# Seven block products in place of eight for h times w_down, in the second half of the rows

## The chip, the cores and the metric

The kernel runs on one core of one Trainium2 chip. The metric is the device time of one execution in microseconds (us); the kernel before took 1466.3 us (median of 3 runs, 1465.88 to 1466.41). The engines are named PE (matrix products; PEld is its loading of weights, the stationary operand), DVE (vector), ACT (scalar), POOL and SP; SP issues nearly all DMAs.

## The reference

With S = 2048 rows, D = 576 and F = 4608, all in float32:

```python
xn = _layernorm(x)                       # x: 1 x 2048 x 576
A  = irfft2(rfft2(xn) * (w_r + 1j * w_i))
h  = sigmoid(xn @ w_gate) * (xn @ w_up)  # 2048 x 4608
out = x + A + h @ w_down                 # w_down: 4608 x 576
```

## The kernel before

**Precision.** A float32 operand is held as two parts, hi and lo, each of which PE multiplies fast. A product is made of three: hi by hi, hi by lo, lo by hi. ACT makes a hi part by a copy, DVE the lo part by a subtraction.

**Staging.** The rows come in two halves of 1024 (`p` = 0, 1), each with two chunks of 512 (`c`) and eight row tiles of 128 (`m`). F comes in 36 blocks of 128 columns (`f`). A unit is one block f of one half: u = 36 p + f, 0 to 71. The normed rows of a half lie transposed in `X`, in hi and lo parts.

**Gate and up.** The first two blocks of each half are made by `plain` (L588), eight block products in two calls. All others are made by `unit` (L607): the 2 x 2 blocks (chunk by half of D, half of D by gate or up) need seven products by sums made beforehand (`PRODS`), each of seven matmuls of 128 x 512 (`prod`, L574, matmul at L576). `unit` puts sigmoid and product together in `y` (128 x 2 x 512), and from y come `hh` and `hl`, the hi and lo parts of h (L662, L663). The four tiles of X that are free are filled with sums beside products that read the others (`fill`, L365).

**Down.** Two units make a pair j = 0 to 17 of each half. `down` (L665) makes for one row tile the product of the pair's h with w_down, twelve matmuls of 128 x 288 (L676) into a pair of PSUM banks; `add` (L679) adds it to `acc` on DVE (L681). The eight row tiles of a pair are spread over the next two units, two after the fifth product of a unit and two after the sixth (`spots`). The pairs of banks (`pair`, L143) are two deep and shared with the spectral part.

**Spectral part.** The transform runs in three stages, `phase1b` (L386), `phase2` (L439) and `phase3` (L483), each of 16 tiles, as generators that are stepped once after each product in units 39 to 71 (`begin`, `aside`). Each issues its loads three steps ahead of its first use.

**Weights.** In the first half, `make_w` and `make_d` (L224, L257) load the raw weights, split them and form their sums, and store the parts in DRAM; in the second half `get_w` (L250) and `get_d` (L269) load the parts. A unit's weights `w` are two deep: unit u + 1's are loaded into the buffer of unit u - 1.

**Order.** `turn` (L811) steps the weights' generators, the additions that are due and the side jobs after each product; `ends` holds the last steps of a unit, which are done in the next one. The framework then orders each engine's instructions by priority and readiness, so that the spectral part's matmuls stand between and inside products. At the end of unit 71, eight row tiles of the last pair remain, each stored as it is done.

Of the kernel before, what the change touches and what calls it, by code (L numbers as in the profile page):

```python
# [33 lines left out]
NX = 7  # L34

# [95 lines left out]
def spectral_glu_kernel(ctx: ExitStack, tc: tile.TileContext, x, w_r, w_i, w_gate, w_up, w_down, out):  # L131
# [38 lines left out]
    wdsp = [tc.dram_tile([P, 2 * D], F32, name=f"wdsp{f}") for f in range(NF)]  # L170

# [5 lines left out]
    accp = ctx.enter_context(tc.tile_pool(name="accp", bufs=1))  # L177
    wpool = ctx.enter_context(tc.tile_pool(name="wpool", bufs=1))
    hp = ctx.enter_context(tc.tile_pool(name="hp", bufs=1))

# [8 lines left out]
    def room(k):  # L189
        fp.close()  # L190
        R["pool"] = pool = fp.enter_context(tc.tile_pool(name=f"p{k}", bufs=1, reuse_waits="tile"))
        return pool
# [30 lines left out]

    def make_w(f):  # L224

        raw = RAW[f]
        WS[f] = w = wpool.tile([P, NX, 5, P], F32R, tag="w", name=f"w{f}", bufs=2)
# [12 lines left out]

    def make_p(f):

        raw = RAW[f]
        WS[f] = w = wpool.tile([P, NX, 5, P], F32R, tag="w", name=f"w{f}", bufs=2)
        for i in (2, 0):
            yield from parts(w, raw[:, i:i + 2], i, 2)
        nc.sync.dma_start(wsp[f][:, :4 * 5 * P], f32(w[:, :4]).rearrange("p a k m -> p (a k m)"))
        yield

    def get_w(u):  # L250
        f = u % NF
        WS[u] = w = wpool.tile([P, NX, 5, P], F32R, tag="w", name=f"w{u}", bufs=2)
        for i in [WB[b] for _, _, b in PRODS] if f >= G else (3, 2, 0, 1):
            nc.sync.dma_start(f32(w[:, i]).rearrange("p k m -> p (k m)"), wsp[f][:, i * 5 * P:(i + 1) * 5 * P])
            yield

    def make_d(f):  # L257
        st = wpool.tile([P, D], F32, tag="std", name=f"std{f}", bufs=1)
        nc.sync.dma_start(st, w_down[f * P:(f + 1) * P, :])
        for _ in range(4):  # L260
            yield
        WD[f] = w = wpool.tile([P, 2, D], F32R, tag="wd", name=f"wd{f}", bufs=4)
        placed(nc.scalar.activation(w[:, 0], st, AF.Copy))
        yield
        nc.vector.tensor_tensor(w[:, 1], st, f32(w[:, 0]), op=OP.subtract)
        nc.sync.dma_start(wdsp[f], f32(w).rearrange("p a d -> p (a d)"))
        yield

    def get_d(u):  # L269
        WD[u] = w = wpool.tile([P, 2, D], F32R, tag="wd", name=f"wd{u}", bufs=4)  # L270
# [83 lines left out]
    def sums(p, m):  # L354
# [5 lines left out]
        rem_parts(p, m, 3, "rm12", 2)  # L360
# [20 lines left out]
    def new_acc(p, m):  # L381
        t = p * TPP + m
        acc[t] = accp.tile([P, D], F32, tag=f"acc{m}", name=f"acc{t}")
# [185 lines left out]
    H = {}  # L569
# [13 lines left out]
    def new_h(u):  # L583
        hh, hl = (hp.tile([P, 2, CW], F32R, tag=k, name=f"{k}{u}", bufs=3) for k in ("hh", "hl"))
# [22 lines left out]
    def unit(u, beside):  # L607


        g, v, y = (hp.tile([P, 2, CW], F32, tag=k, name=f"{k}{u}", bufs=1) for k in ("g", "v", "y"))  # L610
# [31 lines left out]
        hh, hl = new_h(u)  # L642
        if u == LAST - 1:

            nc.vector.tensor_tensor(y[:, 1], y[:, 1], g[:, 1], op=OP.mult)
            nc.scalar.activation(hh[:, 1], y[:, 1], AF.Copy)
            nc.vector.tensor_tensor(hl[:, 1], y[:, 1], f32(hh[:, 1]), op=OP.subtract)
# [3 lines left out]
            nc.scalar.activation(hh[:, 0], y[:, 0], AF.Copy)  # L651
            nc.vector.tensor_tensor(hl[:, 0], y[:, 0], f32(hh[:, 0]), op=OP.subtract)
# [5 lines left out]
        def first():  # L658
# [3 lines left out]
        ends.extend([first, lambda: nc.scalar.activation(hh, y, AF.Copy),  # L662
                     lambda: nc.vector.tensor_tensor(hl, y, f32(hh), op=OP.subtract)])  # L663

    def down(p, j, m):  # L665
# [4 lines left out]
        for g in range(G):  # L670
            u = p * NF + j * G + g
            hh, hl = H[u]
            w = WD[u]
            for l, k in ((hh, 0), (hh, 1), (hl, 0)):
                for b in range(2):
                    nc.tensor.matmul(pd[:, b, :HD], l[:, c, cols], w[:, k, b * HD:(b + 1) * HD],  # L676
                                     start=g == 0 and l is hh and k == 0, stop=g == G - 1 and l is hl)
# [12 lines left out]
        return add  # L690

# [117 lines left out]
    wd = iter(())  # L809

# [14 lines left out]
    for p in range(PAIRS):  # L825
# [38 lines left out]
        for f in range(G, NF):  # L864
            u = p * NF + f

            spots = {4: 2, 5: 2}
            if u + 1 < LAST:
                make = make_w(u + 1) if u + 1 < NF else get_w(u + 1)
            wd = make_d(u) if u < NF else get_d(u)  # L870
# [5 lines left out]
            def beside(i):  # L876
                nonlocal step
                for _ in range(spots.get(i, 0)):
                    if pend:
                        adds.append(down(*pend.pop(0)))  # L880
                if i < 0:
                    return
                turn(2 if u + 1 < NF else 1)
# [6 lines left out]
            finish(make, wd)  # L890
            if u + 2 < NF:
                load_raw(u + 2)
            if f % G == G - 1:

                pend = [(p, f // G, (m + TPC) % TPP if u == LAST - 1 else m) for m in range(TPP)]
# [5 lines left out]
    while pend:  # L901
        down(*pend.pop(0))()
    fp.close()
# [20 lines left out]
```

## Time and profile before

| | |
|---|---|
| time, median of 3 runs | 1466.3 us |
| time of the profiled execution | 1467.37 us |
| its span, first to last instruction | 1465.3 us |
| mean granted TensorE clock | 0.999 |
| HBM read, written | 188.01 MB, 118.42 MB |
| DMA packets, mean rate | 150742, 210 GB/s |

The profile is one execution. A group's row gives line, engine, operation, output and inputs, shapes and count; then its busy time in us and the mean of one in ns; then the idle time of the engine before these instructions, and who ended it. A matmul's end is modelled, and matmuls overlap. A row of a chain gives start, duration and what it was. A row of a stretch (window) gives its limits and length, then for PE, PEld, DVE, ACT and POOL the busy time with the count, then the granted clock, the share of the DMA engines and GB/s. A row of waits gives the total in us, how often, and the longest.

### The profile page before, as it was taken

How to read it: one execution, taken by the hardware profiler on the slowest of the kernel's cores; microseconds unless marked ns; L12 is line 12 of the kernel's file. 1: busy time of each engine (PE TensorE's matmuls, PEld its weight loads, DVE VectorE, ACT ScalarE, POOL GpSimd, SP SyncE). 2: the span in 40 equal slices, each digit the busy share in tenths (PEclk: the TensorE clock that was granted, in tenths of full speed). 3: DMA queues.
4: the chain of work that ended last, by engine and by line, in shares of the span. 5: the costliest groups of instructions: out<-in, count | busy, mean ns of one | idle time of the engine just before them, and what ended most of it. 6: DMA issues, size and time to landing. Idle time of an engine off the chain costs nothing.

```text
span 1465.3 us, 21488 instructions
## 1 busy us (share of the span) xinstructions
PE 1447.4 (99%) x8244; PEld 1275.7 (87%) x8244; DVE 935.7 (64%) x1608; ACT 591.3 (40%) x1021; POOL 5.1 (0%) x21
## 2 busy tenths in 40 slices
PE   7999999999999999999999999999999999999998
PEld 5888888888888888888888888888888889889898
DVE  6888977777777777765455555456666554554544
ACT  5634443444334434453334444434444433333321
POOL 0000000000000000000000000000000000000000
PEclk9999999999999999999999999999999999999999
DMA  6578766666666666666755546477767576744532
GB/s 207 213 258 267 253 225 226 220 217 218 239 235 233 228 223 231 220 206 212 259 179 192 189 155 196 145 229 244 246 217 255 198 246 214 234 158 160 182 109 65
DMA packets 150742, 307.86 MB, mean 210 GB/s; under 512 B 14064, under 2 KB 77808, under 8 KB 145776
## 3 DMA queue, kind: packets, MB, share of 16 engines
q1 hardware_dynamic: 149712, 305.18, 62.0%
q8 instruction: 65, 1.06, 0.3%
q10 hardware_dynamic: 928, 1.31, 0.2%
q14 instruction: 37, 0.30, 0.1%
HBM read 188.01 MB, written 118.42 MB: 209 GB/s over the span
## 4 chain that ended last, share of the span: by engine, by line
PE 92%; DMA 3%; DVE 2%; SPq 1%; ACT 1%; issue 1%; ACTq 0%; DVEq 0%
PE po L676 30%; PE pB L576 22%; PE pE L576 16%; PE pA L576 14%; PE pe L533 2%; PE pd L423 2%; PE pa L434 1%; PE pc L478 1%; PE py L504 1%; PE pb L462 1%; DMA raw<-in_B_w_gate 1%; DMA xt<-in_A_x 0%; PE pz L516 0%; SPq L277 0%; PE pf L408 0%
## 5 line engine op out<-in xcount | busy, mean ns | idle before, releaser
L676 PE MATMUL po<-wd,hh 128*128 128x288 f32 x2304 | 401.7, 296 | 1.6 <-DVE acc L681 1.3
L576 PE MATMUL pB<-X,w 128*128 128x512 f32 x1484 | 381.8, 393 | 1.7 <-ACT w L217 0.9
L681 DVE TENSOR_TENSOR acc<-acc,po 128x576 f32<-128x576 f32 x288 | 215.9, 752 | 226.1 <-PE po L676 225.6
L676 PEld LDWEIGHTS po<-wd,hh 128*128 128x128 f32 x2304 | 343.9, 188 | 16.0 <-DVE acc L681 3.5
L576 PEld LDWEIGHTS pB<-X,w 128*128 128x128 f32 x1484 | 270.8, 188 | 53.5 <-ACT pB L623 1.4
L576 PE MATMUL pE<-X,w 128*128 128x512 f32 x1064 | 274.2, 392 | 0.0
L576 PE MATMUL pA<-X,w 128*128 128x512 f32 x1008 | 260.9, 394 | 0.2 <-DVE X L379 0.2
L676 PE MATMUL po<-wd,hl 128*128 128x288 f32 x1152 | 246.1, 294 | 0.0
L576 PEld LDWEIGHTS pE<-X,w 128*128 128x128 f32 x1064 | 193.2, 188 | 34.4
L576 PEld LDWEIGHTS pA<-X,w 128*128 128x128 f32 x1008 | 188.1, 190 | 37.8 <-DVE X L379 0.7
L676 PEld LDWEIGHTS po<-wd,hl 128*128 128x128 f32 x1152 | 186.4, 189 | 0.0
L217 ACT ACTIVATE w<-raw 128x768 fp32r<-128x768 f32 (+1 forms) x106 | 100.4, 948 | 108.5 <-PE pE L576 88.2
L640 ACT ACTIVATE g<-pB 128x512 f32<-128x512 f32 x68 | 40.6, 598 | 188.1 <-PE pB L576 188.1
L663 DVE TENSOR_TENSOR hl<-y,hh 128x1024 fp32r<-128x1024 f32 x67 | 82.1, 1225 | 31.2 <-ACT hh L662 30.2
L219 DVE TENSOR_TENSOR w<-raw,w 128x512 fp32r<-128x512 f32 (+1 forms) x106 | 81.9, 773 | 5.1 <-ACT w L217 4.7
L660 DVE TENSOR_TENSOR y<-y,g 128x1024 f32<-128x1024 f32 x67 | 82.0, 1224 | 3.6
L662 ACT ACTIVATE hh<-y 128x1024 fp32r<-128x1024 f32 x67 | 70.7, 1055 | 2.8 <-DVE y L660 2.2
L623 ACT ACTIVATE pB<-pA 128x512 f32<-128x512 f32 x68 | 39.6, 582 | 79.5 <-PE pA L576 79.5
L630 ACT ACTIVATE v<-pB 128x512 f32<-128x512 f32 x68 | 40.6, 597 | 67.8 <-PE pB L576 67.5
L637 DVE TENSOR_TENSOR y<-v,pE 128x512 f32<-128x512 f32 x68 | 46.5, 685 | 29.9 <-ACT v L636 28.8
L659 DVE TENSOR_TENSOR y<-v,pE 128x512 f32<-128x512 f32 x67 | 45.9, 685 | 27.6 <-PE pE L576 27.5
L183 DVE TENSOR_TENSOR al<-pd,ah 64x290 fp32r<-64x290 f32 x64 | 29.3, 457 | 40.7 <-ACT ah L182 40.2
(146 smaller groups left out, 1258.4 us busy)
## 6 DMA issues: line engine op xcount, KB each, us to landing
w<-wsp SPq DMA_DIRECT2D x246, 320.0 KB
wsp<-w SPq DMA_DIRECT2D x34, 2240.0 KB
wdsp<-wd SPq DMA_DIRECT2D x36, 576.0 KB
wd<-wdsp SPq DMA_DIRECT2D x36, 576.0 KB
std<-in_B_w_down SPq DMA_DIRECT2D x36, 288.0 KB
raw<-in_B_w_gate SPq DMA_DIRECT2D x72, 128.0 KB
raw<-in_B_w_up SPq DMA_DIRECT2D x72, 128.0 KB
sc<-x SPq DMA_DIRECT2D x16, 290.0 KB
```

The costliest lines, as they stand in the source:

```text
L217: placed(nc.scalar.activation(o[:, :, :3, :], src, AF.Copy))
L219: placed(nc.vector.tensor_tensor(o[:, :, 3:, :], src[:, :, :KT, :], f32(o[:, :, :KT, :]), op=OP.subtract))
L576: nc.tensor.matmul(bank, w[:, sw, :], X[:, x, sx, :], start=start and j == 0, stop=stop and j == len(STEPS) - 1, skip_group_check=skip)
L630: nc.scalar.activation(v[:, 0], bank["B"], AF.Copy)
L637: nc.vector.tensor_tensor(y[:, 1], v[:, 1], bank["E"], op=OP.add)
L640: nc.scalar.activation(g[:, 1], bank["B"], AF.Sigmoid)
L659: nc.vector.tensor_tensor(y[:, 0], v[:, 0], bank["E"], op=OP.add)
L660: nc.vector.tensor_tensor(y, y, g, op=OP.mult)
L662: ends.extend([first, lambda: nc.scalar.activation(hh, y, AF.Copy), lambda: nc.vector.tensor_tensor(hl, y, f32(hh), op=OP.subtract)])
L663: lambda: nc.vector.tensor_tensor(hl, y, f32(hh), op=OP.subtract)])
L676: nc.tensor.matmul(pd[:, b, :HD], l[:, c, cols], w[:, k, b * HD:(b + 1) * HD], start=g == 0 and l is hh and k == 0, stop=g == G - 1 and l ...
L681: nc.vector.tensor_tensor(a, a, pd[:, :, :HD], op=OP.add)
```

## The change

In the second half of the rows, for the pairs j = 1 to 15 (`SEVEN`), h times w_down is made as 2 x 2 blocks (chunk by unit of the pair, unit of the pair by half of D) by seven products. `factor` forms the sums of h in place in the `y` tiles and splits them (`halves`); `make_t` forms the sums of w_down in the first half and stores them in `tsp`. `seven` makes an item in two steps of six matmuls, one step after each product of a unit, and adds it to a running sum: three of the seven go to `acc`, four to `qs`, which `gather` puts together in unit 70. The pairs 0, 16 and 17 of the second half stay with `down`. Unit 38 takes all eight row tiles of pair 0; pair 16 goes to units 70 and 71. Weights of w_down come by block of 128 x 288 (`load_f`).

The buffers are laid out anew: `acc` is one tile, the pools of the spectral part lie on the right side, and a second pool (`lower`) is closed after unit 38 and opened with other tiles. From unit 39 on all units use one tile of `w`: slot by slot, the next unit's weights are loaded into it after the product that read the slot.

```diff
+SEVEN = range(1, NF // G - 2)
...
+    tsp = {j: tc.dram_tile([P, 4 * 2 * HD], F32, name=f"tsp{j}") for j in SEVEN}
...
+    AC = accp.tile([P, TPP, D], F32, name="acc")
...
+    def lower(k):
+        lp.close()
+        L["pool"] = lp.enter_context(tc.tile_pool(name=f"l{k}", bufs=1, reuse_waits="tile"))
...
+    def new_w(u):
+        if u > NF + G:
+            WS[u] = WS[NF + G]
+        else:
+            pool = L["pool"] if u % 2 else wpool
+            WS[u] = pool.tile([P, NX, 5, P], F32R, tag="w", name=f"w{u}", bufs=1)
+        return WS[u]
...
+        if g == 1 and j in SEVEN:
+            yield from make_t(j)
+
+    def make_t(j):
+        b = STD[j].rearrange("p g (b d) -> p (g b) d", b=2)
+        t = R["pool"].tile([P, 4, HD], F32, tag="xa", name=f"wt{j}", bufs=TPC)
+        nc.vector.tensor_tensor(t[:, :2], b[:, 1::2], b[:, :2], op=OP.subtract)
+        nc.vector.tensor_tensor(t[:, 2], b[:, 3], t[:, 0], op=OP.subtract)
+        nc.vector.tensor_tensor(t[:, 3], b[:, 2], t[:, 2], op=OP.subtract)
+        yield
+        th, tl = (R["pool"].tile([P, 4, HD], F32R, tag="xa", name=f"{k}{j}", bufs=TPC) for k in ("wth", "wtl"))
+        split(th, tl, t)
+        for i, v in enumerate((th, tl)):
+            nc.sync.dma_start(tsp[j].rearrange("p (k a d) -> p k a d", k=4, a=2)[:, :, i], f32(v))
+        yield
...
+        late_h = u >= NF + G
+        pool, tag = (hp, "y") if not late_h or u % 4 == (NF + G) % 4 else (L["pool"], f"y{u % 4}")
+        Y[u] = y = pool.tile([P, 2, CW], F32, tag=tag, name=f"y{u}", bufs=1)
...
-        ends.extend([first, lambda: nc.scalar.activation(hh, y, AF.Copy),
-                     lambda: nc.vector.tensor_tensor(hl, y, f32(hh), op=OP.subtract)])
+        ends.append(first)
+        if not late_h:
+            hh, hl = new_h(u)
+            ends.extend([lambda: nc.scalar.activation(hh, y, AF.Copy),
+                         lambda: nc.vector.tensor_tensor(hl, y, f32(hh), op=OP.subtract)])
...
+    ROUND = (("A11", "B11", "Q1"), ("A12", "B21", "C11"), ("A22", "T4", "C21"), ("S1", "T1", "Q5"),
+             ("S3", "T3", "Q7"), ("S2", "T2", "Q6"), ("S4", "B22", "C12"))
...
+    def halves(key, name, src):
+        hs = L["pool"].tile([P, 2, CW], F32R, tag="hs", name=name, bufs=4)
+        HS[key] = hs
+        nc.scalar.activation(hs[:, 0], src, AF.Copy)
+        return lambda: nc.vector.tensor_tensor(hs[:, 1], src, f32(hs[:, 0]), op=OP.subtract)
...
+    def load_f(key, name, src):
+        WF[key] = w = L["pool"].tile([P, 2, HD], F32R, tag="wf", name=name, bufs=6)
+        nc.sync.dma_start(f32(w), src)
...
+    def factor(n):
...
+        put, a, b, op = {"S1": ("A22", "A21", "A22", OP.add), "S3": ("A21", "A11", "A21", OP.subtract),
+                         "S2": ("A11", "A22", "A11", OP.subtract), "S4": ("A12", "A12", "A11", OP.subtract)}.get(nm, (nm,) * 4)
+        if put != nm:
+            nc.vector.tensor_tensor(A[put], A[a], A[b], op=op)
+        return halves((j, k), f"hs{j}_{k}", A[put])
...
+    def seven():
+        QS["q"] = L["pool"].tile([P, 4, TPC, HD], F32, name="qs")
...
+        for n, (j, k) in enumerate(ITEMS):
+            h, w, nm = HS[j, k], WF[j, k], ROUND[k][2]
+            for mm in range(2):
+                pd = pair(f"ps{j}_{k}_{mm}")
+                for i in range(2):
+                    m = slice((2 * mm + i) * P, (2 * mm + i + 1) * P)
+                    for q, (a, b) in enumerate(((0, 0), (0, 1), (1, 0))):
+                        nc.tensor.matmul(pd[:, i, :HD], h[:, a, m], w[:, b], start=q == 0, stop=q == 2)
+                if mm == 0:
+                    load_item(n + 2)
+                    low = factor(n + 1)
+                else:
+                    low()
+                o = sums_of(nm, mm)
+                if nm[0] == "Q" and j == SEVEN[0]:
+                    nc.scalar.activation(o, pd[:, :, :HD], AF.Copy)
+                else:
+                    nc.vector.tensor_tensor(o, o, pd[:, :, :HD], op=OP.add)
+                yield
...
+    def gather():
...
+            nc.vector.tensor_tensor(o, a, b, op=OP.add)
+            yield
...
+            if u == NF + G:
+                spots = {3: 2, 4: 2, 5: 2, 6: 2}
+            elif u == LAST - 2:
+                spots = {i: 1 for i in range(2, 7)}
+                pend = [(p, f // G - 1, m) for m in range(TPP)]
+                sides.append(gather())
+            elif u == LAST - 1:
+                spots = {i: 1 for i in range(3)}
...
-            wd = make_d(u) if u < NF else get_d(u)
+            wd = make_d(u) if u < NF else iter(())
...
+                if (u, i) == (NF + G + 1, 5):
+                    rounds = seven()
...
+                if u > NF + G:
+                    next(rounds, None)
```

More of the change, by code (lines that the diff above doesn't have):

```diff
@@ L190, in room @@
         fp.close()
-        R["pool"] = pool = fp.enter_context(tc.tile_pool(name=f"p{k}", bufs=1, reuse_waits="tile"))
+        R["pool"] = pool = fp.enter_context(tc.tile_pool(name=f"p{k}", bufs=1, side="right", reuse_waits="tile"))
         return pool
@@ L222, in parts @@
         yield
+    def new_w(u):
[5 more added lines that the diff above has]
+        return WS[u]
     def make_w(f):
         raw = RAW[f]
-        WS[f] = w = wpool.tile([P, NX, 5, P], F32R, tag="w", name=f"w{f}", bufs=2)
+        w = new_w(f)
         B12, B22, B21, B11 = (raw[:, i] for i in range(4))
@@ L243, in make_p @@
         raw = RAW[f]
-        WS[f] = w = wpool.tile([P, NX, 5, P], F32R, tag="w", name=f"w{f}", bufs=2)
+        w = new_w(f)
         for i in (2, 0):
@@ L251, in get_w @@
         f = u % NF
-        WS[u] = w = wpool.tile([P, NX, 5, P], F32R, tag="w", name=f"w{u}", bufs=2)
+        w = new_w(u)
         for i in [WB[b] for _, _, b in PRODS] if f >= G else (3, 2, 0, 1):
@@ L257, in make_d @@
     def make_d(f):
-        st = wpool.tile([P, D], F32, tag="std", name=f"std{f}", bufs=1)
+        j, g = divmod(f, G)
+        if g == 0:
+            STD[j] = L["pool"].tile([P, G, D], F32, tag="std", name=f"std{j}", bufs=1)
+        st = STD[j][:, g]
         nc.sync.dma_start(st, w_down[f * P:(f + 1) * P, :])
-        for _ in range(4):
+        for _ in range(3):
             yield
-        WD[f] = w = wpool.tile([P, 2, D], F32R, tag="wd", name=f"wd{f}", bufs=4)
+        WD[f] = w = L["pool"].tile([P, 2, D], F32R, tag="wd", name=f"wd{f}", bufs=4)
         placed(nc.scalar.activation(w[:, 0], st, AF.Copy))
@@ L382, in new_acc @@
         t = p * TPP + m
-        acc[t] = accp.tile([P, D], F32, tag=f"acc{m}", name=f"acc{t}")
+        acc[t] = AC[:, m]
         load_x(acc[t], t)
@@ L583, in new_h @@
     def new_h(u):
-        hh, hl = (hp.tile([P, 2, CW], F32R, tag=k, name=f"{k}{u}", bufs=3) for k in ("hh", "hl"))
+        hh, hl = (L["pool"].tile([P, 2, CW], F32R, tag=k, name=f"{k}{u}", bufs=3) for k in ("hh", "hl"))
         H[u] = (hh, hl)
@@ L876, in beside @@
             def beside(i):
-                nonlocal step
+                nonlocal step, rounds
+                if (u, i) == (NF + G + 1, 5):
+                    rounds = seven()
                 for _ in range(spots.get(i, 0)):
@@ L880, in beside @@
                         adds.append(down(*pend.pop(0)))
+                for a in extra.get((u, i), ()):
+                    a()
                 if i < 0:
                     return
+                if u > NF + G:
+                    next(rounds, None)
                 turn(2 if u + 1 < NF else 1)
@@ L890, in spectral_glu_kernel @@
             finish(make, wd)
+            if u == NF + G:
+                lower("b")
             if u + 2 < NF:
                 load_raw(u + 2)
-            if f % G == G - 1:
-                pend = [(p, f // G, (m + TPC) % TPP if u == LAST - 1 else m) for m in range(TPP)]
+            if p == 0 and f % G == G - 1:
+                pend = [(p, f // G, m) for m in range(TPP)]
+    pend = [(PAIRS - 1, NF // G - 1, (m + TPC) % TPP) for m in range(TPP)]
     for e in ends:
```

82 lines of the change are left out of this document (68 added, 14 removed).

## The prediction

> **What bounds the kernel now.** I read the page first, then the chain of work that ended last, then PE's timeline, and last the stretches (windows) of DVE, the engine to which the change gives work.
>
> ```profile
> span 1465.3 us, 21488 instructions
> PE 1447.4 (99%) x8244; PEld 1275.7 (87%) x8244; DVE 935.7 (64%) x1608; ACT 591.3 (40%) x1021; POOL 5.1 (0%) x21
> ...
> PE 92%; DMA 3%; DVE 2%; SPq 1%; ACT 1%; issue 1%; ACTq 0%; DVEq 0%
> ...
> L676 PE MATMUL po<-wd,hh 128*128 128x288 f32 x2304 | 401.7, 296 | 1.6 <-DVE acc L681 1.3
> ...
> L681 DVE TENSOR_TENSOR acc<-acc,po 128x576 f32<-128x576 f32 x288 | 215.9, 752 | 226.1 <-PE po L676 225.6
> ```
>
> PE is busy for 99% and is 92% of the chain: what PE no longer does comes off the end, unless something else is late. But a matmul's 296 ns is no price: 8244 matmuls share 1447.4 us, so 176 ns each, though the narrow ones are shown with 296 ns. They overlap, and the cost is the distance between starts. The chain merges a block of h times w_down of 24 matmuls, and PE's timeline near the end shows products without other work between them:
>
> ```profile
> 246.62 3.18 PE po L676 x24
> ...
> 281.66 3.18 PE po L676 x24
> ```
>
> ```profile
> 1435.01 1.75 PE L576 MATMUL pA<-X,w 128*128 128x512 f32 x7
> 1436.60 1.75 PE L576 MATMUL pB<-X,w 128*128 128x512 f32 x7
> 1438.19 0.69 PE L676 MATMUL po<-wd,hh 128*128 128x288 f32 x4
> ...
> 1441.37 1.77 PE L576 MATMUL pB<-X,w 128*128 128x512 f32 x7
> 1442.98 0.69 PE L676 MATMUL po<-wd,hh 128*128 128x288 f32 x4
> ```
>
> 24 matmuls in 3.18 us are 0.1325 us each, not 0.296. A gate/up product of seven takes 1.59 us from start to start beside another product (1435.01 to 1436.60, and to 1438.19), 1.61 us between two blocks of h times w_down (1441.37 to 1442.98). The period of two units in the first half of the rows is 281.66 - 246.62 = 35.04 us; 14 products at 1.59 and 96 narrow matmuls at 0.1325 make 22.3 + 12.7 = 35.0. So there PE has no slack at all, and the prices 1.59 and 0.1325 are good.
>
> **The change part by part.** *Fewer matmuls.* For one pair of units (a j), the second half computed 8 row tiles of 12 matmuls, 96; now 7 products of 2 x 2 x 3, 84, of the same width and the same weight loads. 12 fewer, in 15 of the 18 pairs (SEVEN): 180 x 0.1325 = 23.9 us off PE. Taken from the 296 ns it would be 53 us, which the overlap forbids.
>
> The Trainium skill, "TensorE: Matmul & The Clock Gate", section "Back-to-back issue gap", puts a lone warm matmul at N/2.4 + 2.5 ns, 122.5 ns for 288 columns; the trace's 132.5 differs from it, and by the page the saving would be 180 x 0.1225 = 22.1 us. The sum goes by the trace.
>
> *Smaller groups.* In place of two blocks of 24 per unit, PE gets seven blocks of 6, each between two gate/up products. From the rows above, a product between two foreign blocks costs 1.61 and beside its own kind 1.59, so up to 5 products per unit become 0.02 dearer: 5 x 0.02 x 30 units = 3 us at most, and 0 at least, since phases of the spectral part already stand between products. I take 2.
>
> *Accumulation and sums on DVE, and copies on ACT.* Rows:
>
> ```profile
> L663 DVE TENSOR_TENSOR hl<-y,hh 128x1024 fp32r<-128x1024 f32 x67 | 82.1, 1225 | 31.2 <-ACT hh L662 30.2
> L470 DVE TENSOR_TENSOR t<-wi,sw 128x512 f32<-128x512 f32 x16 | 11.0, 686 | 0.0
> L662 ACT ACTIVATE hh<-y 128x1024 fp32r<-128x1024 f32 x67 | 70.7, 1055 | 2.8 <-DVE y L660 2.2
> L604 ACT ACTIVATE hh<-y 128x512 fp32r<-128x512 f32 x8 | 5.0, 629 | 7.3 <-DVE y L603 7.3
> ```
>
> Per pair, DVE before: 8 additions x 0.752 + 2 lower parts x 1.225 = 8.5 us. After: 14 additions x 0.752 (a product goes out in two, of 576 elements each, like before), 4 sums of h x 0.686, 7 lower parts x 0.686 = 18.1 us. That is 9.6 us more per pair, 4.8 per unit. ACT: 7 x 0.629 in place of 2 x 1.055, 2.3 us more per pair of some 42 us; ACT is at 40%, and each copy is made a step ahead, so I cost it at nothing; without that cover it would be 0.63 us per item. The eight additions of 1152 elements that put the running sums together (twice 0.75, some 1.4 us each, an estimate from the 576 row) lie in the last unit but one, one per step, off PE's path. Now the stretches of DVE, the first two of the first half, the others of the second half by the stage of the spectral part beside it, and then the second blocks of units 38 and 71 in the chain:
>
> ```profile
> 300.00:400.00 100.00, 100.00 (x550) 88.57 (x550) 75.06 (x104) 42.35 (x59) 0.00 (x0) 1.00 0.64 222
> 75.00:185.00 110.00, 109.04 (x598) 96.01 (x597) 98.69 (x250) 46.65 (x64) 0.00 (x0) 1.00 0.77 258
> 740.00:960.00 220.00, 219.30 (x1289) 190.45 (x1288) 120.27 (x207) 90.06 (x194) 1.19 (x12) 1.00 0.53 174
> 1000.00:1150.00 150.00, 149.82 (x845) 130.72 (x844) 93.76 (x172) 68.38 (x107) 0.00 (x0) 1.00 0.74 236
> 1190.00:1400.00 210.00, 210.00 (x1261) 188.12 (x1260) 106.82 (x172) 73.71 (x151) 0.00 (x0) 1.00 0.55 185
> ```
>
> ```profile
> 733.24 3.19 PE po L676 x24
> ...
> 1443.14 3.18 PE po L676 x24
> ```
>
> ```profile
> DVE al L183 <- ACT ah L182: 40.2, 48, 2.6
> DVE acc L681 <- PE po L676: 29.0, 25, 2.4
> ```
>
> ```profile
> DVE acc L681 <- PE po L676: 24.7, 20, 2.4
> DVE z L469 <- ACT sw L465: 17.3, 11, 3.1
> ```
>
> ```profile
> DVE acc L681 <- PE po L676: 37.6, 37, 2.4
> ```
>
> (The waits are those of the three last stretches, in their order.) The two blocks are 33 units apart, 709.9/33 = 21.5 us per unit in the mean. The 4.8 us more per unit are 0.223 of it, and the shorter unit is 0.963 of the old one. DVE's busy share is 120.27/220 = 0.547 in the first stage, then 0.625 and 0.509; with 0.223 it is 0.770, 0.848 and 0.732, below 0.963. By busy time alone DVE keeps room, and the cost is 0. The other end counts all idle time that is not a wait for h times w_down as if DVE could do nothing in it: 220 - 120.27 - 29.0 = 70.7, then 31.5 and 65.6 us. Then the shares are (120.27 + 70.7)/220 + 0.223 = 1.091, 1.058 and 1.044, that is 0.128, 0.095 and 0.081 more than there is; over stages of some 220 us each, 67 us are lost. Most of that idle time is DVE waiting for ACT in the middle of a chain (al for ah, z for sw) with nothing else in its queue; now it has the sums and the lower parts, which are ready, and when DVE is behind ACT is done before it asks. So I take a value near the first end: 8 us, with 0 and 67 kept for the range.
>
> *The queue behind a wait.* The new waits: the lower part of an item on DVE waits for ACT's copy; behind it stand that step's addition and the spectral part's work, and PE waits for both, for the lower part as weights one step later, and for the addition because the two pairs of PSUM banks are shared. A step is 1.6 + 0.8 us or more, the lower part and an addition 1.44, so the cover holds while DVE is under a microsecond late; this is what the 8 us stand for.
>
> *Weights in one buffer.* From unit 39 on each slot of w is loaded for the next unit as soon as its product is done, and needed a unit minus a product later, some 19 us. The nearest landings:
>
> ```profile
> 748.06 4.26 DMA xb<-in_A_x
> ...
> 961.68 6.46 DMA x<-sc
> ```
>
> ```profile
> SPq L254 <- PE pE L576: 136.2, 32, 13.6
> ```
>
> 4.3 to 6.5 us hide in 19. SP already waits for PE before it loads weights (the last row), now once per product; behind it stand the loads of the spectral part, which the program issues three steps, some 9 us, ahead of use: hidden again, and 0 taken. If SP fell 4 us behind, a stage's load would cost up to 2 us in each of 48 tiles; I keep a few us for it in the range. The seven loads of 295 KB blocks per pair add 0.9 MB to some 42 us, 21 GB/s beside 236.
>
> *First half.* make_t adds, per pair, 0.75 for 576 elements, at most 0.69 each for two times 288, and 1.225 x 1152/1024 = 1.4 for the lower part, 3.5 us at most to DVE, one copy of 1152 elements to ACT and two stores of 590 KB. DVE is at 75% in the run of the first half, but in 75 to 185 us at 98.69 of 110, where three pairs lie: 3 x 3.5 = 10 us if all of it reached PE, 0 if lateness is made up from 185 us on. PE's largest wait for DVE in the whole trace is small, so most is made up, and I take 2:
>
> ```profile
> PEld po L676 <- DVE acc L681: 3.5, 5, 1.1
> ```
>
> The stores add 1.18 MB to 35 us, 34 GB/s beside 258 at a DMA share of 0.77 there, about 0.87 then: hidden, and if not, inside the same 10 us.
>
> *Edges.* Unit 39 and the end of unit 71 lose the blocks that covered the copy of a bank (0.6 us by the ACT row of 0.629) before the product that overwrites it: 1 us. New tags, one acc tile and the new sides of the pools take nothing away from any engine: 0, as the fill of X's slots beside products that read other slots shows for parts of one tile.
>
> *Sum.* 1467.4 (the profiled execution's own time, 2.1 above its span) - 23.9 + 2 + 8 + 2 + 1 = 1456.5. The median of the runs is 1.1 below the profiled one: **1455.4 us**.
>
> **The rivals.** *Nothing comes back* (chance 0.14): DVE fills its idle time and only the fewer matmuls count, 1466.3 - 23.9 = 1442.4. For it: PE's largest wait for DVE is the 3.5 us above; the program's scheduler mixes products and phases freely. Against it: the groups get smaller and DVE reaches 85% in one stage.
>
> *DVE sets the pace in the second half* (0.20, slower): half of the 67 us stay, 33 us. 1466.3 - 23.9 + 5 + 33 = 1480.4. It decides from 18.9 us on, that is 0.63 us per unit, or 28% of the 67 us. For it: additions grow from 8 to 14 per pair and PE's pairs of banks are two deep. Against it: 225.6 of DVE's idle us were waits for PE's own blocks.
>
> *The gains are just used up* (0.07): the losses come to 21 to 27 us; 1466.
>
> *One weight buffer stops PE* (0.01): if loads for the next unit had to wait for the whole tile, PE would stand for a landing, 4.3 us or more in each of 32 units, 140 us, 1580 us. Against it: loads and products name single slots. The Trainium skill, "Trainium Kernel Development and Optimization", section "Best Practices", asks for double buffers so that loads lie beside compute; by that rule this change goes the wrong way, and no row of this trace shows a single weight buffer.
>
> **How the numbers follow.** My forecast, 1455 with some cost, has 0.58. A measurement tells about 0.2%, 3 us, from no change. Faster by more: 0.58 + 0.14 = 0.72. Within it: 0.07. Slower: 0.21. The range goes from 1439 (nothing lost, and 3 us of the small gaps in the second half, now with a block after every product, filled) to 1480 (the pace of DVE). The forecast's own range is 1446 to 1462.
>
> **What would show it.** Matmuls of L676 and of the rounds together down by 180 to 8064 in all, at the same 0.1325 us apart; DVE at about 1120 us busy; the period of two units up to unit 37 still 35.04. In the second half a unit 0.3 to 0.8 us shorter. Wrong, if PE shows waits for the lower parts or for the additions of more than 15 us in all, if units of the second half grow, or if stalls show in 75 to 185 us.

## The result and the profile after

The changed kernel took 1456.87 us (median of 4 runs, 1455.53 to 1457.43) against 1466.12 us for the kernel before on the same chip: a ratio of 0.9935, 95% interval 0.9918 to 0.9953. The forecast was 1455.4 us. The profiled execution took 1457.23 us, with a span of 1454.9 us. First the page of the changed kernel: span, busy time, chain and groups.

```profile
span 1454.9 us, 21987 instructions
...
PE 1429.5 (98%) x8064; PEld 1252.7 (86%) x8064; DVE 1100.4 (76%) x1896; ACT 645.3 (44%) x1122; POOL 4.9 (0%) x21
...
L726 PE MATMUL po<-wd,hh 128*128 128x288 f32 x1216 | 212.8, 297 | 4.5 <-DVE acc L730 4.4
L817 PE MATMUL ps<-wf,hs 128*128 128x288 f32 x1260 | 202.1, 295 | 0.0
...
L827 DVE TENSOR_TENSOR qs<-qs,ps 128x576 f32<-128x576 f32 x112 | 84.1, 751 | 31.6 <-PE ps L817 30.7
L827 DVE TENSOR_TENSOR acc<-acc,ps 128x576 f32<-128x576 f32 x90 | 67.6, 751 | 33.3 <-PE ps L817 32.6
L754 DVE TENSOR_TENSOR hs<-y,hs 128x512 fp32r<-128x512 f32 x105 | 71.5, 687 | 2.9 <-ACT hs L753 1.9
```

PE has 180 matmuls fewer, and the seven products (L817) never kept it idle (0.0). DVE has 165 us more and still waits for PE, not PE for it, in the additions to the running sums. The only idle time of PE in these rows stands at L726, the old code, of which most runs in the first half of the rows.

The chain in the third stage of the spectral part shows the new pattern:

```profile
1314.66 0.80 PE ps L817 x6
1315.45 1.60 PE pB L619 x7
1317.05 0.80 PE ps L817 x6
1317.85 1.60 PE pA L619 x7
```

Six narrow matmuls between two products take 0.80 us, 0.1325 each as in the old blocks of 24, and a product between two of them takes 1.60.

The next table is worked out from the two traces and from those of the experiments: the time between the first gate/up matmuls of two units, which splits the execution into stretches that hold the same work in all kernels, but for the matmuls saved. "End" is the start of the last matmul.

```
units            2-11    12-17   18-37   38-47   48-59   60-end
before          180.15  105.12  361.53  232.15  248.95  278.94
after           184.98  108.71  363.02  229.64  238.53  271.48
difference       +4.83   +3.59   +1.49   -2.51  -10.42   -7.46
```

The first half of the rows lost 10 us (unit 38 starts at 710.55 us, before at 700.38), the second half gained 20.4. The forecast had 2 lost and 12.9 gained: two errors of about 8 us that cancel. All times here count from the span's first instruction. The expectations below count unit 38 from the zero of each trace's own clock, 10.6 to 11.5 us earlier, so that their 721.5 is this 710.55; a second number in brackets is in their count. The windows of the first half, after and then before, show the loss on PE:

```profile
75.00:185.00 110.00, 107.94 (x588) 93.53 (x587) 95.19 (x210) 46.61 (x63) 0.00 (x0) 1.00 0.77 254
190.00:425.00 235.00, 231.99 (x1265) 201.73 (x1263) 191.05 (x300) 103.05 (x139) 0.00 (x0) 1.00 0.76 260
```

```profile
190.00:425.00 235.00, 235.00 (x1312) 209.30 (x1311) 172.20 (x240) 94.60 (x132) 0.00 (x0) 1.00 0.66 231
```

From 190 to 425 us PE was never idle before and issued 47 matmuls more in the same time. DVE is at 191 of 235 us there, so it isn't full; what it waits for, and who then waits for it, the waits of the whole execution say (engine, line and tile, what was waited for: us in total, times, longest):

```profile
DVE wt L302 <- DMA std<-in_B_w_down: 13.5, 9, 3.5
PEld po L726 <- DVE acc L730: 10.7, 18, 1.4
PE po L726 <- DVE acc L730: 4.7, 9, 1.0
...
PEld ps L817 <- DVE acc L827: 0.4, 2, 0.2
PEld ps L817 <- DVE qs L827: 0.2, 1, 0.2
PEld ps L817 <- DVE hs L754: 0.2, 1, 0.2
```

One such place, in the timelines of SP's queue, then of DVE and PE (start, duration, what; in brackets the idle time ahead and its releaser):

```profile
293.71 1.98 SPq L286 DMA_DIRECT2D std<-in_B_w_down  x1
...
311.79 0.57 SPq L309 DMA_DIRECT2D tsp<-wth  x1
313.80 0.55 SPq L309 DMA_DIRECT2D tsp<-wtl  x1
314.40 1.35 SPq L286 DMA_DIRECT2D std<-in_B_w_down  x1
```

```profile
300.11 0.76 DVE L302 TENSOR_TENSOR wt<-std 128x576 f32<-128x576 f32 x1 [2.46 <-DMA std<-in_B_w_down]
...
306.59 0.75 DVE L730 TENSOR_TENSOR acc<-acc,po 128x576 f32<-128x576 f32 x1
...
307.40 0.79 PE L726 MATMUL po<-wd,hh 128*128 128x288 f32 x4 [0.60 <-DVE acc L730]
```

The raw block of w_down that `make_t` needs is issued at 293.71 us and there at 300.1. DVE stands still for 2.46 us in front of it, with the lower parts of the weights and the additions queued behind. The addition that frees a pair of PSUM banks comes late, and PE waits. In SP's queue the next raw block (314.40) stands behind the two new stores, which themselves wait until ACT and DVE have made the parts.

### The profile page after: what moved, and what is told of

Read it like the earlier page. It is cut to its first block, busy times and chain, and to the rows that moved or that the text cites. A ratio compares the mean times of both kernels' runs of the same rounds, so it can differ in the third digit from the quotient of the medians.

```text
span 1454.9 us, 21987 instructions
## 1 busy us (share of the span) xinstructions
PE 1429.5 (98%) x8064; PEld 1252.7 (86%) x8064; DVE 1100.4 (76%) x1896; ACT 645.3 (44%) x1122; POOL 4.9 (0%) x21
## 5 line engine op out<-in xcount | busy, mean ns | idle before, releaser
L726 PE MATMUL po<-wd,hh 128*128 128x288 f32 x1216 | 212.8, 297 | 4.5 <-DVE acc L730 4.4
L817 PE MATMUL ps<-wf,hs 128*128 128x288 f32 x1260 | 202.1, 295 | 0.0
L817 PEld LDWEIGHTS ps<-wf,hs 128*128 128x128 f32 x1260 | 187.6, 188 | 15.3 <-ACT u L523 1.2
L726 PEld LDWEIGHTS po<-wd,hh 128*128 128x128 f32 x1216 | 180.9, 188 | 15.8 <-DVE acc L730 10.1
L730 DVE TENSOR_TENSOR acc<-acc,po 128x576 f32<-128x576 f32 x168 | 125.6, 752 | 70.4 <-PE po L726 68.8
L726 PE MATMUL po<-wd,hl 128*128 128x288 f32 x608 | 129.8, 295 | 0.0
L827 DVE TENSOR_TENSOR qs<-qs,ps 128x576 f32<-128x576 f32 x112 | 84.1, 751 | 31.6 <-PE ps L817 30.7
L726 PEld LDWEIGHTS po<-wd,hl 128*128 128x128 f32 x608 | 98.1, 189 | 0.6 <-DVE hl L710 0.5
L827 DVE TENSOR_TENSOR acc<-acc,ps 128x576 f32<-128x576 f32 x90 | 67.6, 751 | 33.3 <-PE ps L817 32.6
L754 DVE TENSOR_TENSOR hs<-y,hs 128x512 fp32r<-128x512 f32 x105 | 71.5, 687 | 2.9 <-ACT hs L753 1.9
```

The source lines that it names most:

```text
L726: nc.tensor.matmul(pd[:, b, :HD], h[i], w[k][b], start=g == 0 and n == 0, stop=g == G - 1 and n == 2)
L730: nc.vector.tensor_tensor(a, a, pd[:, :, :HD], op=OP.add)
L754: return lambda: nc.vector.tensor_tensor(hs[:, 1], src, f32(hs[:, 0]), op=OP.subtract)
L817: nc.tensor.matmul(pd[:, i, :HD], h[:, a, m], w[:, b], start=q == 0, stop=q == 2)
L827: nc.vector.tensor_tensor(o, o, pd[:, :, :HD], op=OP.add)
```

## The experiments

The theory so far: the first half's 10 us are the work of `make_t`, which reaches PE through DVE; the second half pays nothing for DVE. Rivals: the stores cost it and not DVE's own work; and, for the second half, that DVE does set the pace and the fewer matmuls are worth more than 23.9 us. Times are medians, with the ratio to runs of the kernel before on the same chip.

**Without the items' preparation.** `make_t` is left out, and the T items load plain blocks of w_down, so the sums of w_down are not part of what is computed.

```diff
-        if g == 1 and j in SEVEN:
-            yield from make_t(j)
...
```

> The changed kernel without make_t: no sums of w_down are formed or stored in the first half, and the items with T1 to T4 load plain blocks of w_down of the same size in their place. Theory (make_t's work on DVE makes the additions late, and PE waits for the shared banks): unit 38 starts at 711 to 712 us in place of 721.5, the first half has the period 35.04 us throughout, and the time is 1447, 10 us below the changed kernel. Rival (the new layout of the buffers and the new order of the instructions cost the 10 us, whatever make_t does): unit 38 at 721, time 1457. A rival about the stores alone expects 1447 here too.

Measured: 1449.75 us, ratio 0.989 [0.9877, 0.9904]; unit 38 at 701.01 us (711.90), and from unit 4 on every two units up to 34 take 35.04 again. So the whole 10 us are `make_t`'s, but only 7.1 us of them reach the end: units 38 to the end then take 741.9 us against 739.7 of the changed kernel.

**The work without the stores.** The parts are made, and not stored; the T items load plain blocks.

```diff
-        for i, v in enumerate((th, tl)):
-            nc.sync.dma_start(tsp[j]..., f32(v))
...
```

> The changed kernel with make_t's sums, copy and lower part on DVE and ACT as they are, but without its two stores; the items with T1 to T4 load plain blocks in their place. Theory (DVE's work): unit 38 still starts at 719 to 722 us, time 1456 to 1457. Rival (the stores hold up SP and the DMA engines, so that the loads of w_down come late and stop DVE): unit 38 at 711 to 713, time 1447 to 1449.

Measured: 1451.84 us, ratio 0.9903 [0.9889, 0.9916]; unit 38 at 702.91 (713.68). Units 2 to 37 take 2.1 us more than before. So all of DVE's and ACT's added work costs 2.1 us of the first half, the stores with all that they hold up the other 7.8. The theory as first put falls; the time lies between its range and the rival's.

**The work on POOL.** The four vector operations of `make_t` go from DVE to POOL.

```diff
-        nc.vector.tensor_tensor(t[:, :2], b[:, 1::2], b[:, :2], op=OP.subtract)
+        nc.gpsimd.tensor_tensor(t[:, :2], b[:, 1::2], b[:, :2], op=OP.subtract)
...
-        split(th, tl, t)
+        split(th, tl, t, nc.gpsimd)
```

> The changed kernel with make_t's four vector operations on POOL in place of DVE, everything else as it is; the output is the reference's. Theory (DVE's work): unit 38 at 712 to 714 us, time 1447 to 1449, even if POOL takes several us for each operation, since nothing but the stores waits for it. Rival (stores, SP or the layout): unit 38 at 721, time 1457. A second rival: POOL slows DVE while both work, time above 1452.

Measured: 1490.96 us, ratio 1.0168 [1.0154, 1.0182], slower; unit 38 at 745.44 (756.16). A group of POOL and one of DVE in this kernel, then the same two operations on DVE in the changed kernel:

```profile
L302 POOL TENSOR_TENSOR wt<-std 128x576 f32<-128x576 f32 x15 | 23.7, 1579 | 468.0 <-DMA std<-in_B_w_down 386.9 <-DMA raw<-in_B_w_up 58.4 <-DVE raw L257 22.7
L292 DVE TENSOR_TENSOR wd<-std,wd 128x576 fp32r<-128x576 f32 x36 | 32.1, 893 | 9.0 <-ACT wd L290 8.8
```

```profile
L302 DVE TENSOR_TENSOR wt<-std 128x576 f32<-128x576 f32 x15 | 11.4, 757 | 13.7 <-DMA std<-in_B_w_down 13.5
L292 DVE TENSOR_TENSOR wd<-std,wd 128x576 fp32r<-128x576 f32 x36 | 27.2, 755 | 1.3 <-ACT wd L290 0.8
```

POOL takes 1579 ns where DVE took 757, and DVE's own operations become longer (755 to 893 ns in the mean). The Trainium skill, "GPSIMD Engine Reference", section "Engine selection", advises against elementwise work of two inputs there, at about half of DVE's speed: the rows agree, 2.1 times. Its section "Specifications" names an SBUF interface shared with DVE; the longer DVE rows fit it.

These longer operations are not all of the 34 us: in this kernel the granted clock also falls beside some of PE's waits for DVE. One such wait, with the first matmuls behind it, and the window that follows (the granted clock is the third number from the end):

```profile
92.36 1.33 PE L726 MATMUL po<-wd,hh 128*128 128x288 f32 x4 [2.93 <-DVE acc L730]
```

```profile
91.60:98.40 6.80, 6.04 (x25) 6.04 (x26) 4.54 (x11) 0.83 (x2) 0.00 (x0) 0.50 0.79 313
```

The 24 narrow matmuls from 92.36 us take 5.92 us to the next product (98.28), where they take 3.18 at the full clock. This kernel has five stretches at a granted clock of 0.50 between 91 and 317 us, 20.5 us in all, which cost half of that, some 10 us (an estimate); the changed kernel has none between unit 2 and its last matmul. Each begins beside a pause of PE of 1.8 to 2.9 us, but pauses of 1.87 and 2.40 us (at 116.31 and 267.05) have none behind them, so no threshold follows from these traces. How the rest of the 34 us divides between DVE's longer operations and loads that stand behind the later stores is not shown.

**The price of 180 matmuls.** The kernel before, with one of the three matmul groups (hi of h by lo of w_down) left out for the first block of a pair in six of eight row tiles, pairs 1 to 15 of the second half: 180 narrow matmuls fewer and nothing else.

```diff
-            for l, k in ((hh, 0), (hh, 1), (hl, 0)):
+            few = p == 1 and 1 <= j <= 15 and g == 0 and m not in (2, 6)
+            for l, k in ((hh, 0), (hl, 0)) if few else ((hh, 0), (hh, 1), (hl, 0)):
```

> The kernel before, with 12 of the 96 narrow matmuls of a pair left out in pairs 1 to 15 of the second half (one of the three parts in one of the two units of six of the eight row tiles), 180 matmuls in all, and nothing else. It measures what 180 matmuls are worth by themselves. By the distance between starts, 0.1325 us each: 1466.1 - 23.9 = 1442 us. By the durations that the profile shows, 0.296 us: 1413. If PE were not what sets the time in the second half: 1460 to 1466.

Measured: 1443.42 us, ratio 0.9845 [0.9831, 0.9858]; 22.65 us, or 0.126 us each by the medians, 24.1 over units 38 to the end by the two traces. The price of the forecast stands.

**The stores later.** A pair's two stores are issued a unit later, after the load of the next raw block.

```diff
+        while LATE:
+            LATE.pop(0)()
...
-        for i, v in enumerate((th, tl)):
-            nc.sync.dma_start(tsp[j]..., f32(v))
+        def put():
+            for i, v in enumerate((th, tl)):
+                nc.sync.dma_start(tsp[j]..., f32(v))
+        LATE.append(put)
```

> The changed kernel with the two stores of make_t issued a unit later, behind the next unit's load of w_down, when their data have long been ready; the output is the reference's. Theory now (the stores make SP wait for ACT and DVE, and the loads of w_down and of the raw weights behind them come late, which stops DVE): the time falls to that without stores, 1451 to 1453 us, unit 38 at 713 to 715. Rival A (the 17.7 MB that the stores write slow the loads, whoever issues them and when): 1456 to 1457, unit 38 at 720 to 722.

Measured: 1464.28 us, ratio 0.999 [0.9982, 0.9999]; unit 38 at 716.52 (727.53), 6 us worse than the changed kernel. The expectation failed. The raw block that came earlier is the first of a pair: it is issued at 310.79 us, in front of the stores at 311.99 and 313.98, where the changed kernel issues it at 314.40 behind them. But the sums wait for both blocks, and the load of the second, which stands behind the stores in both kernels, now comes later: in the odd units 25 to 33 it is issued 0.8 to 1.2 us after its unit begins, in the changed kernel 1.1 to 1.5 us before. DVE's sums waited 15.4 us for raw blocks between 185 and 640 us, against 8.1 in the changed kernel, and the loss went on until 640 us, 0.3 to 2 us in most second units.

**The stores on POOL's queue.** With that, nothing new stands in SP's.

```diff
-            nc.sync.dma_start(tsp[j]..., f32(v))
+            nc.gpsimd.dma_start(tsp[j]..., f32(v))
```

> The changed kernel with the two stores of make_t issued by POOL, which has nothing else to do, in place of SP; same traffic at the same moments. Theory (SP held up): 1451 to 1453 us. Rival A (traffic): 1456 to 1457. Rival B (POOL's work on the stores slows DVE, as its arithmetic did): above 1457.

Measured: 1456.31 us, ratio 0.9929 [0.9916, 0.9943]; unit 38 at 708.45 (719.98). The time is the one that rival A names, but the loss moved: 7.2 us in units 2 to 11, none from unit 12 on. So SP's order explains what is lost later, and not what is lost early.

**DVE's work doubled in the second half.** The lower part of each of the 105 items is made twice.

```diff
                 else:
                     low()
+                    low()
```

> The changed kernel with the lower part of each item made twice on DVE in the second half, 105 operations of 0.69 us more, 2.4 us per unit; the output is the reference's. If DVE has room there, as forecast (share 0.85 at most, 0.96 with this), the time rises by 0 to 8 us, to 1457 to 1465. Rival (DVE all but sets the pace in the second half): each us on DVE costs at least half on PE, 36 us or more, 1493 and up.

Measured: 1454.31 us, ratio 0.9916 [0.9902, 0.9929]. The windows of units 49 on of this kernel:

```profile
960.00:1180.00 220.00, 219.87 (x1229) 192.31 (x1228) 201.40 (x357) 105.85 (x176) 0.00 (x0) 1.00 0.88 268
1180.00:1400.00 220.00, 219.62 (x1291) 195.93 (x1290) 177.73 (x297) 90.61 (x191) 0.00 (x0) 1.00 0.71 213
```

With DVE at 201.4 of 220 us, PE is still at 219.87. In units 48 to 59 the doubled work costs nothing, from unit 60 on 1.6 us (the table at the end of this section). By the medians the whole kernel is even 2.6 us faster than the changed one, below both ranges (the intervals of the two ratios overlap): units 38 to 47 take 4.3 us less, and why is not shown. DVE does not set the pace of the second half.

**One weight buffer in the kernel before.** From unit 39 on all units use one tile of `w`, as in the change, with all else as before.

```diff
-        WS[u] = w = wpool.tile([P, NX, 5, P], F32R, tag="w", name=f"w{u}", bufs=2)
+        if u > NF + G:
+            WS[u] = w = WS[NF + G]
+        else:
+            WS[u] = w = wpool.tile([P, NX, 5, P], F32R, tag="w", name=f"w{u}", bufs=2)
```

> The kernel before with one part of the change alone: from unit 39 on all units use one tile for the gate and up weights, and the next unit's loads go into a slot after its product. As forecast (19 us to land in, 4.3 to 6.5 needed; the other loads not held up): 1466, within 1.5 us. Rival (SP, tied to each product, issues the spectral part's loads too late): 1470 or more, with waits of DVE for xb and of ACT for x2 and u. Rival (the tile is waited for as a whole): 1580 or more.

Measured: 1474.46 us, ratio 1.0056 [1.004, 1.0071], 8 us slower, as the first rival has it. All of it lies in units 38 to 47, beside the first stage of the spectral part: 240.45 us against 232.15; units 48 to 59 and 60 to the end take 248.28 and 278.85, as before. SP's waits for products between 740 and 960 us, then the place of PE's longest wait there (timelines of DVE, ACT and PE, and the window behind it):

```profile
SPq L257 <- PE pB L579: 44.5, 19, 6.3
SPq L257 <- PE pE L579: 31.1, 13, 5.0
...
SPq L257 <- PE pA L579: 24.3, 16, 2.7
```

```profile
902.39 0.58 DVE L317 TENSOR_SCALAR xb<-xb,mv,rstd 128x576 f32<-128x576 f32 x1 [3.08 <-DMA xb<-in_A_x]
903.50 0.41 ACT L182 ACTIVATE ah<-pd 64x290 fp32r<-64x290 f32 x1 [3.44 <-DVE al L183]
903.96 0.40 PE L437 MATMUL pa<-ah,am 128*128 128x290 f32 x1 [2.33 <-ACT ah L182]
```

```profile
905.00:908.40 3.40, 3.40 (x16) 3.40 (x15) 0.65 (x2) 0.66 (x1) 0.00 (x0) 0.50 0.52 164
```

SP waited for products before weight loads in 7 places before (33.1 us), and now does so once per product (100 us); its waits in all have hardly grown (165 us against 154), but now the loads of the stage stand between them. DVE's waits for the blocks of x come to 11.4 us, 7.3 before. In the place shown DVE stands in front of such a block, `al` stands ready behind it on DVE, ACT waits for `al`, and PE for ACT; then the granted clock is 0.50 for 3.4 us, which costs another 1.7 (an estimate). That the blocks come late by their place in SP's queue is read from the order of the loads; no run separates it. The Trainium skill's rule on double buffers ("Trainium Kernel Development and Optimization", "Best Practices") has the right sign here, by 8 us and not by a landing per unit: the weights themselves were in time, the loads of another stream were not.

**The raw blocks early; the weights late; both.** Three kernels from the changed one. In the first, both raw blocks of a pair are loaded at the pair's first unit, ahead of the stores; in the second, each slot's load of gate/up weights is issued two steps later.

```diff
+            for k in range(G):
+                nc.sync.dma_start(STD[j][:, k], w_down[(f + k) * P:(f + k + 1) * P, :])
         st = STD[j][:, g]
-        nc.sync.dma_start(st, w_down[f * P:(f + 1) * P, :])
```

```diff
         w = new_w(u)
+        if u > NF + G:
+            yield
+            yield
...
```

> The kernel after, with the two raw blocks of w_down of a pair loaded together at the pair's first unit, so that the second block's load no longer stands on SP's queue behind the stores of the first item, which wait for ACT's and VectorE's parts. Theory 'the late raw block stops VectorE, and the additions behind it make TensorE wait': the loss after about 280 us goes away, unit 38 starts at 714 to 717 us (721.5 in the kernel after, 711.9 without the items' work), no wait of a VectorE `wt` for the raw block over 2 us in 185 to 430 us, and 1451 to 1453.5 us in all. Rival 'the stores' traffic itself, or VectorE's order of work, costs the 7.6 us whatever the load's place': unit 38 stays at 720 to 722 us and the time at 1456 to 1457.5.

> The kernel after, with each load of a slot of the single gate and up buffer issued two steps later than now in the second half, so that SP waits less for the product that reads the slot and is free for the loads of the spectral blocks. Theory 'one buffer ties SP to each product, and loads of other streams come late': the units of 740 to 960 us take 2 to 4 us less in all, SP's waits for products at the slots' loads get shorter, and 1453 to 1455 us in all. Rival 'that stage's 3 us are something else': no change, 1456.5 to 1457.5 us. Third: the later weights themselves come too late for the next unit's first products, PE waits for w, and it is slower than 1458.

> Both edits of the two kernels before it at once. If the two losses are separate, their gains add: by the theories 1448 to 1451 us, by the rivals 1456 to 1457. Unit 38 as in the first of them, 740 to 960 us as in the second.

Measured: 1455.65 us (ratio 0.9924 [0.9907, 0.994]), 1456.87 (0.9934 [0.9919, 0.9949]) and 1454.79 (0.9921 [0.9906, 0.9936]). The first did what the theory says from 280 us on, and only there. Its waits between 75 and 280 us, and its window after that:

```profile
PEld po L727 <- DVE acc L731: 7.2, 6, 2.3
...
PE po L727 <- DVE acc L731: 5.0, 3, 1.9
...
DVE wt L303 <- DMA std<-in_B_w_down: 1.2, 1, 1.2
```

```profile
280.00:430.00 150.00, 150.00 (x832) 133.23 (x831) 122.41 (x173) 66.72 (x91) 0.00 (x0) 1.00 0.77 266
```

PE is never idle there any more, and units 12 to 17 take 105.12 us as before the change. The gain is only 1.2 us by the medians. But units 2 to 11 now lose 7.7 us, 1.1 to 2.2 in each of the units 3, 5, 7, 9 and 11, those in which `make_t` stands; unit 38 starts at 708.43 us (719.42, not 714 to 717). One place of it, in unit 5, in the timelines of ACT, DVE and PE:

```profile
118.89 1.17 ACT L231 ACTIVATE w<-raw 128x1152 fp32r<-128x1152 f32 x1 [1.70 <-DMA raw<-in_B_w_gate]
120.10 0.96 DVE L233 TENSOR_TENSOR w<-raw,w 128x768 fp32r<-128x768 f32 x1 [2.16 <-ACT w L231]
...
125.60 0.76 DVE L731 TENSOR_TENSOR acc<-acc,po 128x576 f32<-128x576 f32 x1
```

```profile
126.41 0.80 PE L727 MATMUL po<-wd,hh 128*128 128x288 f32 x4 [1.89 <-DVE acc L731]
```

It is the same chain with another load at its head: the raw blocks of gate and up for the next unit. SP issues them from 105.06 us on, behind two stores at 84.65 and 93.59 us for which it stood still; in the next kernel below, which has no such stores there, from 94.70 on. Between 75 and 280 us SP waits 32 us at the new stores here, and DVE waits 9.5 us for ACT's copies of raw weights (3.4 before the change). By this place, SP's order still costs something in the first units when the blocks of w_down are early.

The second edit changed nothing, SP's waits for products neither (40.5, 32.8 and 30.5 us against 39.9, 32.7 and 30.9): it did not take away what it was meant to, so it tells nothing about the 3 us of that stage. Both edits together lie between the two ranges; that kernel has 3.4 us at a granted clock of 0.50 at 164.3 us, behind a pause of PE of 2.1 us.

**The first items made late.** What is left lies where DVE has the later statistics and the backlog of the start beside the items. So the raw blocks early, and the items 1 to 5 made in the units 14, 20, 26, 32 and 34 from blocks loaded once more.

```diff
+        if g == 1 and j in SEVEN and j > len(LATER):
+            yield from make_t(j)
+        if f in LATER:
+            yield from make_t(1 + LATER.index(f), again=True)
+
+    LATER = (14, 20, 26, 32, 34)
...
```

> The kernel after, with the two raw blocks of w_down of a pair loaded together (this alone: loss of 8.1 us up to unit 38, all of it in the units 3, 5, 7, 9 and 11, where an item is made while VectorE still has the later statistics and a backlog), and with the items 1 to 5 made later, in the units 14, 20, 26, 32 and 34, from blocks of w_down that are loaded once more. Theory 'an item costs 1 to 2 us only where VectorE is full': the units 3 to 11 keep the times of before, the later items cost 0 to 0.5 us each, unit 38 starts at 711.5 to 714 us, and 1447 to 1451 us in all. Rival 'an item costs its 1 to 2 us wherever it stands in a unit with other work of w_down' : the loss moves to the units 14 to 34, unit 38 at 718 to 722 us, 1454 to 1458 us in all. Neither: the five more loads take DMA time that the stores need, and later items start to cost as well: over 1458.

Measured: 1449.08 us (1448.65 to 1450.0), ratio 0.9881 [0.9865, 0.9898]: as the theory has it. It is the fastest version that leaves nothing out, 7.8 us ahead of the changed kernel, 6.6 of them by the later items. Waits between 75 and 430 us, and windows:

```profile
PEld po L738 <- DVE acc L742: 1.7, 1, 1.7
PE po L738 <- DVE acc L742: 1.3, 1, 1.3
DVE wt L314 <- DMA std<-in_B_w_down: 0.7, 2, 0.4
```

```profile
280.00:430.00 150.00, 150.00 (x834) 133.33 (x834) 123.84 (x175) 67.29 (x90) 0.00 (x0) 1.00 0.80 276
430.00:640.00 210.00, 210.00 (x1165) 186.56 (x1164) 170.08 (x240) 92.57 (x125) 0.00 (x0) 1.00 0.77 268
```

The same items, with 2.95 MB more to load, show no cost from unit 2 on: units 2 to 37 take 646.94 us, before 646.80, and unit 38 starts at 701.36 (711.96).

The stretches of these kernels, in us, as in the table above:

```
units                    2-11    12-17   18-37   38-47   48-59   60-end
before                  180.15  105.12  361.53  232.15  248.95  278.94
180 matmuls fewer       180.26  105.12  361.53  226.39  238.56  271.03
one weight buffer       180.49  105.12  361.50  240.45  248.28  278.85
after                   184.98  108.71  363.02  229.64  238.53  271.48
no items' preparation   180.02  105.12  361.85  230.99  239.45  271.45
no stores               182.17  105.31  361.39  232.11  239.03  271.43
work on POOL            204.30  115.53  371.77  231.20  238.51  271.45
stores later            185.29  108.65  369.15  230.59  238.57  271.44
stores on POOL's queue  187.30  105.14  361.43  231.44  238.82  271.47
lower parts twice       184.93  108.72  362.89  225.35  237.66  273.12
raw blocks early        187.84  105.12  361.61  230.37  238.64  271.48
weights late            185.10  108.60  362.93  229.26  238.55  271.46
both                    188.77  105.12  361.45  228.64  238.88  271.52
first items late        180.31  105.12  361.51  230.68  238.71  271.45
```

## Why the prediction was right, and where only its sum was

By the medians the change is: 22.65 us gained by 180 matmuls fewer; 5.7 lost in the second half and by a preparation that nothing is in the way of (1449.08 against 1443.42; by the traces 4.3 of it in units 38 to 47); 7.8 lost in the first half by where that preparation stands (1456.87 against 1449.08). The forecast had 23.9, 11 and 2.

- **Fewer matmuls.** Right: 22.65 us where 23.9 was taken from the starts in the timeline; the 53 us by the shown durations would have been far off. The Trainium skill's figure for a matmul by itself ("TensorE: Matmul & The Clock Gate", "Back-to-back issue gap") gave 22.1 (an estimate); the medians lie between the two, the 24.1 us of the traces a little above both.
- **Smaller groups.** 2 us taken. Six matmuls still take 0.80 us, a product between two of them 1.60, and units 48 to 59 are as short as in the kernel that only has fewer matmuls (238.53 and 238.56): about 0.
- **DVE in the second half.** 8 us taken, 67 kept as the other end. From unit 48 on the trace has 0.4 us more than with the fewer matmuls alone, and with 105 operations more on DVE, some 72 us in all of the second half, 0.8 us more than that. DVE's idle time was there to be filled, as the text argued against its own rival; the 8 us and the rival (0.20) priced a thing that does not happen. The row that spoke against them, DVE's waits for PE's own blocks, should have weighed more.
- **Weights in one buffer.** "Hidden again, and 0 taken" was wrong in kind: in the kernel before, the single buffer alone costs 8 us, by the waits through loads of the spectral part that come late on SP's queue. In the changed kernel the same stage (units 38 to 47) is 3.3 us longer than with the fewer matmuls alone. That these 3.3 us are the buffer's is not shown. The kernel with the lower parts made twice has the same buffer and takes 225.35 us there, 1 us less than with the fewer matmuls alone; the kernels that change only the first half (POOL, stores later, stores on POOL's queue, raw blocks early, first items late) take 230.37 to 231.44; and the edit aimed at the buffer did not reach SP's waits. It stays open.
- **First half.** The mis-sized term: 2 us taken, 10 measured in the trace, 7.8 by the medians against the late items. The steps that failed are "0 if lateness is made up from 185 us on", with "so most is made up, and I take 2", and for the stores "hidden". DVE's share told nothing of its order: it stood still in front of a raw block while additions that were ready to go waited behind. The step priced the stores as traffic and did not follow SP's queue, where the next raw block stands behind them. With the blocks early, nothing is lost from unit 12 on; with the first items late as well, nothing in units 2 to 11. In those first units the loss is not one thing. Without stores it is 2.0 us. With the raw blocks early it is 7.7, and the place shown has SP's order at its head once more, by the raw blocks of gate and up. With the stores on POOL's queue it is 7.2, though they don't hold up SP: there ACT waits 7.5 us between 75 and 280 us for raw blocks of w_down, DVE 3.8 for the same and 3.9 for blocks of x, and DVE is busy for 100.65 of 110 us from 75 to 185 us. Whether the stores' traffic makes these loads late (the DMA share is 0.93 from 130 to 185 us, 0.75 before the change) is argued, not shown.
- **The marks.** 8064 matmuls and 0.60 us less per unit in the second half (20.4 us over 34 units) came as put; DVE's 1100 us is near the 1120, though the prediction's own terms (9.6 and 3.5 us in each of 15 pairs, and eight additions of 1.4) add up to 1143. The period of 35.04 did not hold. The marks for "wrong" were in part met: PE's waits for additions come to 15.4 us with those of its weight loads, and PE lost 1.1 us in 75 to 185 us. They pointed at the first half, and rightly. That the total came out within 1.5 us was luck: the 8 us too many in the second half made up for the 8 too few in the first.

## What to carry to other kernels

When work is moved into an earlier phase "beside" other work, write down for each queue it enters what stands behind it: a vector instruction that waits for a load stops every ready instruction behind it, and a store that waits for a result stops the next load; busy shares show neither. Then put such work in a stretch that has room for it, even if its input must be loaded twice: here that was worth 6.6 us. Price a buffer made single also by what shares the DMA queue with its loads, not only by whether its own data come in time.

## What the runs showed that was not expected

- A vector engine at 201.4 of 220 us busy did not slow a PE that was at 219.87, with additions on two-deep banks between them.
- POOL's subtractions take 2.1 times DVE's time (1579 and 757 ns) and lengthen DVE's at the same time (755 to 893 ns in the mean): taking the items' 45 us (in the changed kernel 20.2 for the lower parts and 25 for the sums) off DVE made the kernel 34 us slower than the changed one.
- Stores moved later made things worse (1464.28 us against 1456.87): the first raw block of a pair came earlier, but the second, for which the sums also wait, came later.
- A pause of PE can cost more than its length: in three kernels (POOL, one weight buffer, both edits) the granted clock was 0.50 for 3.4 or 6.8 us beside pauses of 1.8 to 2.9 us.
